# An adaLN block on one core: the scale columns loaded ahead of the shift columns, the first key projection in token halves, eight single PSUM banks, and a new written-out order

## The chip, the core and the metric

The kernel runs on one core of a Trainium2 chip. The metric is the time of one execution on the device in microseconds; the number given for a kernel is the median of several runs. A profile is one execution taken by the hardware profiler; its span runs from the first to the last instruction of the program. TensorE is called PE below, VectorE DVE, ScalarE ACT, GpSimd POOL, and SyncE, which issues most of the DMAs here, SP.

## What is computed

```python
def reference(A_x, A_wqkv, A_wo, B_x, B_w1, B_b1, B_w2, B_b2, c, w_mod):
    def _A_ref(x, wqkv, wo):          # H = 32 heads of 16, W = 8 keys, dilation 2
        q, k, v = split(x @ wqkv)
        idx = pos[:, None] - off[None, :]            # off = 0, 2, .., 14
        logits = einsum('bhsd,bhswd->bhsw', q, k[idx]) * scale   # idx < 0 masked
        o = einsum('bhsw,bhswd->bhsd', softmax(logits), v[idx])
        return o.reshape(B, S, D) @ wo
    def _B_ref(x, w1, b1, w2, b2):    # mixes tokens: S = 2048, F = 1792
        u = gelu(einsum('bsd,sf->bdf', layernorm(x), w1) + b1)
        return transpose(einsum('bdf,fs->bds', u, w2) + b2)
    mod = silu(c) @ w_mod             # six rows of 512: sa, ca, ga, sb, cb, gb
    h = layernorm(x) * (1 + ca) + sa
    x = x + ga * _A_ref(h, A_wqkv, A_wo)
    h = layernorm(x) * (1 + cb) + sb
    return x + gb * _B_ref(h, B_w1, B_b1, B_w2, B_b2)
```

x is 2048 x 512 in bfloat16, wqkv 512 x 1536, wo 512 x 512, w1 2048 x 1792, w2 1792 x 2048, w_mod 512 x 3072.

## The kernel before

The 2048 tokens are worked in four chunks of 512 (`build_chunk`, L562), each of four tiles of 128 tokens. Nothing is scheduled while the kernel runs: the function records some 670 operations in a graph (`_Graph`, L98), and the string `ORDER` (L27) names them one by one. An engine gets its operations in the order in which their names stand there, and works them off strictly in that order; a suffix chooses the engine where an operation has alternatives (`:v` DVE, `:a` ACT, `:g` POOL), and a digit the PSUM buffer where it takes one. So where an operation waits, all later ones of that engine wait behind it. The order of names of different engines against each other means nothing on the chip. A `dur` beside an operation, such as 0.95 for `gmul` on POOL (L548), is the author's number and isn't used when the program runs.

The operations of chunk n, by the names that the text uses:

- `ln1s`, `rstd1_n`, `nb1_n`, `ln1n`: statistics of the first layernorm by tile of 128 tokens (`ln1s0` to `ln1s15`), the reciprocal deviation, minus mean times it, and the normalized tile. `nb1_n` and `ln1n` may run on POOL. An `ln1n` on ACT or POOL needs `nb1_n`.
- `tr`, `hT`: PE transposes the normalized tiles into PSUM; the eviction multiplies by 1 + ca and adds sa (`a1col`, `sacol`).
- `qkvk`, `qkvq`, `qkvv` and `evk`, `evq`, `evv`: projections, and their evictions to SBUF.
- `vd`: 16 SP DMAs copy the values into the shifted layout.
- `qk` (four per chunk): DVE multiplies queries and eight shifted keys, 4096 elements per partition, both inputs from SBUF. `red` sums over the head's elements on PE with column tiles, `max` (DVE, from PSUM), `sub` (PE), `exp` (ACT), `sum` (PE), `rb` (ACT), `smul` (DVE) finish the softmax.
- `a2`, `a2ev`, `pv` (four, like `qk`, DVE, both inputs from SBUF), `pvacc` (PE, column tiles), `oev`: the weighted values.
- `wo`, `x1ev`, `x1sq`: output projection per tile, with the residual. It needs `woq` multiplied by the row ga: `bc0` (SP) spreads the row over the partitions into `ga_bc`, and `gmul0` to `gmul3` multiply the four 512-wide parts of `woq` (L545 to L551), each on DVE or on POOL.
- `t`, `aff`, `ln3s`, `h3`: second layernorm, its scale and shift, and the third layernorm. `t` and `h3` may run on POOL.

Then `mlp1` multiplies by w1 in two halves of tokens (the first half is parked in SBUF, `park`, and is ready after two chunks, so its matmuls fill PE's time during chunks 2 and 3), `gadd`, `gelu` and `gbm` follow, and `mlp2`, `xb`, `fin` and `st_out` finish.

At the start, two DMAs, `ld_wmodA` and `ld_wmodB`, bring the columns of both sa and ca of w_mod by halves of rows (L413, L414). `modcols0` and `modcols1` multiply them with silu(c), and `modcols_cp` writes `sacol` and `a1col` (L482 to L503). `warm0` to `warm4` are 21 matmuls whose results nobody reads. PSUM is four tiles of two banks each (L273); an operation that fills one bank still holds both. Eight semaphores are shared by all DMAs of SP and ACT, so the issue of a DMA waits for the landing of the eighth one before it.

Of the kernel before, what the change touches and what calls it, by code (L numbers as in the profile page):

```python
# [27 lines left out]
consts ld_x00 consts2 ld_c warm0:0 ld_x02 ld_wmodA act_table ld_wmodB ld_w1a ld_x1a cps:1 warm1:2 ld_w1b silu_exp  # L28
ln1s0:v ld_x1b ln1s1:a ld_x2 ld_w0 silu_dve halo0 warm2:3 ln1s2:v rstd1_0_0 ln1s3:v modcols0:0 nb1_0_0:v ln1n0:v
warm3:1 rstd1_0_2 ln1n1:v nb1_0_2:v ln1n2:v modcols1 ln1n3:v tr0_00:2 tr0_10:3 modcols_cp:a tr0_02 tr0_12 hT0_0:a  # L30
warm4:1 hT0_1:v hT0_3:v qkvk0_0:0 hT0_2:v sc_rep ln1s7:v ln1s4:v ln1s9:v ln1s8:v ln1s11:v ln1s10:v qkvk0_1:1 qkvk0_2:3
qkvk0_0b qkvk0_1b ln1s5:a ln1s6:a rstd1_1_0 evk0_1:a nb1_1_0:g qkvq0_1:2 qkvq0_0:1 evk0_2:a evk0_0:a evq0_1:a ln1n7:a
evq0_0:a ln1n6:g ln1n4:g ln1n5:v qk0_1 qk0_0 qkvq0_2:3 ld_wo3 ld_wmod2 ld_w2 ld_wo1 ld_wmod3 ld_x3 ld_wmod4 ld_wmod5
ld_wo2 khalo1 ld_wo0 evq0_2:a tr1_10:0 tr1_00:2 qkvv0_0:1 qkvv0_2:3 hT1_0:a hT1_1:a hT1_3:a hT1_2:a evv0_0:a evv0_2:a
rstd1_2_0 vd0_010 vd0_030 vd0_020 vd0_120 vd0_000 vd0_021 vd0_001 vd0_031 vd0_100 vd0_101 vd0_131 vd0_011 vhalo1
vd0_130 ld_b2 vd0_111 vd0_121 vd0_110 qkvk1_0:0 qkvq1_0:2 red0_0:1 qk0_2 qk0_3 nb1_2_0:v red0_1 red0_2 red0_3 ln1s13:v
ln1s12:v max0 qkvq1_2:3 sub0 ln1n10:g ln1n11:g ln1n8:g evk1_0:a ln1s15:a ln1n9:a evq1_0:a ln1s14:a rstd1_3_0 evq1_2:a
exp0 qkvk1_2:0 modrows:2 tr2_10:3 sum0 evk1_2:a mrow_ev rb0 qk1_1 qk1_0 qk1_3 smul0 nb1_3_0:v qk1_2 tr2_00:0 qkvv1_0:2
a2_0:1 hT2_0:a hT2_1:a hT2_2:a ln1n12:a a2ev0:a evv1_0:a hT2_3:a ln1n15:a ln1n13:a ln1n14:a pv0_0 pv0_1 qkvv1_2:0
red1_0:1 red1_1 red1_2 red1_3 qkvq2_0:2 tr3_00:3 evv1_2:a evq2_0:a hT3_0:a bc0 khalo2 vd1_030 vd1_120 vd1_020 vd1_021  # L40
vd1_010 vd1_000 vd1_001 vd1_100 vd1_031 vd1_110 vd1_011 vd1_131 vd1_130 vd1_111 vd1_121 vd1_101 pvacc0_0:0 pvacc0_1
qkvk2_0:2 max1 pv0_3 pv0_2 oev0_1:a hT3_2:a sub1 tr3_10:0 qkvv2_0:3 evk2_0:a exp1 sum1 pvacc0_2:2 hT3_1:a rb1 hT3_3:a
gmul3:g gmul0:v gmul2:v gmul1:v qk2_1 smul1 qk2_0 pvacc0_3 qkvv2_2:1 oev0_3:a evv2_0:a evv2_2:a wo1:0 a2_1:2 x1ev1:a
a2ev1:a pv1_0 pv1_1 wo3:3 wo0:1 wo2:0 x1ev3:a x1sq1 x1sq3 x1ev0:a x1ev2:a qkvk2_2:2 pvacc1_0:3 qkvq2_2:1 pvacc1_1
x1sq2 evk2_2:a x1sq0 rstd2_0_0 evq2_2:a pv1_2 nb2_0_0:v pv1_3 t0:v qk2_3 qk2_2 qkvq3_0:0 pvacc1_2:2 pvacc1_3 qkvk3_0:1
t2:a t3:a oev1_1:a evq3_0:a oev1_3:a t1:a wo6:3 wo7:0 wo5:2 evk3_0:a x1ev6:a vhalo2 ld_b1 bc2 ld_w1_0_1 khalo3 bc1
vd2_101 ld_w1_0_2 vd2_000 ld_w1_0_0 vd2_131 vd2_121 vd2_010 vd2_001 vd2_030 vd2_031 ld_w1_0_3 vd2_020 red2_0:1 red2_1
wo4:3 x1sq6 x1ev7:a x1ev5:a x1sq7 x1sq5 x1ev4:a x1sq4 rstd2_1_0 red2_2 red2_3 aff0_0 qk3_1 ln3s0_1:v nb2_1_0:v
ln3s0_3:a max2 ln3s0_0:v ln3s0_2:v qkvv3_2:0 qkvk3_2:2 sub2 t4:a t7:g t6:g t5:g evv3_2:a exp2 rstd3_0_0 evk3_2:a
aff1_0 nb3_0_0:v qkvv3_0:3 biascols:0 sum2 qkvq3_2:2 rb2 h3_3:a evv3_0:a evq3_2:a ln3s1_2:a ln3s1_3:a h3_1:g h3_0:g  # L50
ln3s1_0:v biascols_cp ln3s1_1:v h3_2:v qk3_0 smul2 qk3_2 rstd3_1_0 mlp1_0_30_0:1 mlp1_0_31_0 mlp1_0_10_0:0 mlp1_0_11_0
a2_2:3 red3_0:2 red3_1 a2ev2:a nb3_1_0:v qk3_3 h3_6:a h3_4:a h3_5:a h3_7:v red3_2 mlp1_0_00_0:3 mlp1_0_01_0 red3_3
# [24 lines left out]
st_out14_0 st_out15_384
# [20 lines left out]
class _Graph:  # L98
# [11 lines left out]
    def slot(self, pool):  # L110
        return _Slot(pool)
# [36 lines left out]
    def schedule(self):  # L148
# [3 lines left out]
        for tok in ORDER.split():  # L152
            name, _, how = tok.partition(":")
            o = by[name]
            if how and how[0].isalpha():
                o.eng, o.dur, o.fn = next(a for a in o.alts if a[0] == ENGINES[how[0]])
                how = how[1:]
            assert done.issuperset(o.deps), name
            for s_ in o.use:
                if s_.first == o.idx:  # L160
                    s_.i = int(how)
                    assert busy[s_.pool][s_.i] is None, name
                    busy[s_.pool][s_.i] = s_
# [68 lines left out]
def kernel(  # L232
# [14 lines left out]
    WARM=(4, 4, 4, 5, 4),  # L247
# [63 lines left out]
    sacol = T([P, KT], F32, "sacol")  # L311
# [669 lines left out]
```

## Time and profile before

| | |
|---|---|
| median of 3 runs | 198.21 us (198.18 to 198.45) |
| the profiled execution, span | 197.0 us |
| what lies around the span in the median | 1.2 us |
| DVE, ACT, POOL busy over the span | 153.5, 123.4, 18.0 us |
| first matmul, end of the last one | 1.4 us, 194.1 us |
| granted TensorE clock, mean | 0.998 |

How to read it: a row of a timeline gives the start, the duration of the whole group, engine, line, operation, tiles written and read, shapes, and the number of instructions; the bracket is the idle time of the engine before it and what ended it. All operations pass through one helper, so that nearly every row has its line, L184, and is told apart by its tiles: `ps<-hTb,w_q` is a query projection, `prod<-q_sb,k_c`, `gT<-q_sb,k_c` and `h<-q_sb,k_c` are `qk`, `pvb<-a2sb,vD` is `pv`, `ee<-ps` is `exp`, `ps<-ee,ident` is `sum`, `ee<-ee,rb` is `smul`, `woq<-woq,ga_bc` is `gmul`, `n_sb<-xx,...` is `ln1n`, `junk<-xx` with `junk<-xx,mv` is `ln1s` on ACT, and `h<-h,...` is `h3`. Matmuls are pipelined, so a PE row overlaps the next one; the distance of starts is what counts.

### The profile page before, as it was taken

What the parts mean: (1) busy time and instruction counts of PE and PEld (TensorE: products, weight loads), DVE (VectorE), ACT (ScalarE), POOL (GpSimd) and SP (SyncE); (2) the same over time, 40 slices, a digit from 0 to 9 for tenths busy, and PEclk for the clock granted to TensorE, in tenths of its full rate; (3) what the DMA queues carried; (4) which work ended last, traced back from release to release, by engine and by line L of the source; (5) the groups of instructions that cost most, each with busy time, mean ns of one, the idle gap of its engine ahead of it and who ended that gap; (6) DMA issues with size and microseconds to landing.
All of it is one profiled execution on the core that took longest, in us unless ns stands there. A gap on an engine that the chain in (4) does not pass through costs nothing.

```text
span 197.0 us, 3408 instructions
## 1 busy us (share of the span) xinstructions
PE 190.1 (97%) x1289; PEld 88.2 (45%) x1289; DVE 153.5 (78%) x198; ACT 123.4 (63%) x242; POOL 18.0 (9%) x46
## 2 busy tenths in 40 slices
PE   7889999999999999999999999999999999999994
PEld 2546545445443435433434444444444444444452
DVE  1699989999999999999999999928776127261463
ACT  5498999999999999993769999917541000000000
POOL 7003040090000004300000011000000000000000
PEclk9999999999999999999999999999999999999999
DMA  6999978507994994693999999990000871720112
GB/s 182 369 312 318 302 195 177 120 14 180 171 196 99 270 201 84 187 289 106 174 206 290 234 295 292 292 273 4 0 0 0 229 200 68 199 81 26 57 53 80
DMA packets 45348, 33.59 MB, mean 171 GB/s; under 512 B 5396, under 2 KB 42772, under 8 KB 45332
## 3 DMA queue, kind: packets, MB, share of 16 engines
q1 hardware_dynamic: 44908, 32.82, 67.2%
q10 hardware_dynamic: 424, 0.56, 1.0%
q8 instruction: 10, 0.16, 0.4%
q14 instruction: 6, 0.05, 0.1%
HBM read 22.03 MB, written 2.10 MB: 122 GB/s over the span
## 4 chain that ended last, share of the span: by engine, by line
PE 64%; DVE 12%; DMA 11%; ACT 5%; SPq 3%; issue 2%; ACTq 0%; DVEq 0%
PE ps L184 64%; DMA vD<-v_c 5%; DMA w_q<-in_A_wqkv_dram 4%; SPq L184 3%; DVE pvb L184 3%; DVE prod L184 3%; DMA vD<-in_w_mod_dram 3%; DVE st L184 2%; ACT n_sb L184 1%; DVE h L184 1%; ACT hTb L184 1%; DVE gT L184 1%; ACT v_c L184 1%; DVE ee L184 1%; DVE nm L184 1%
## 5 line engine op out<-in xcount | busy, mean ns | idle before, releaser
L184 DVE TENSOR_TENSOR pvb<-a2sb,vD 128x4096 bf16<-128x4096 bf16 x16 | 36.0, 2284 | 0.2 <-issue 0.2
L184 PE MATMUL ps<-h,wst 128*128 128x512 bf16 x128 | 29.5, 379 | 0.0
L184 DVE TENSOR_TENSOR prod<-q_sb,k_c 128x4096 bf16<-128x4096 bf16 x9 | 20.4, 2285 | 0.1
L184 PEld LDWEIGHTS <-wst 128*128 128x128 bf16 x128 | 12.1, 98 | 16.0 <-issue 1.7
L184 PE MATMUL ps<-gT,vD 128*128 128x512 bf16 x84 | 19.1, 379 | 0.0
L184 PE MATMUL ps<-hTb,w_q 128*128 128x512 bf16 x64 | 15.1, 381 | 1.0 <-DMA w_q<-in_A_wqkv_dram 0.7
L184 DVE TENSOR_TENSOR q_sb<-ps,q_sb 128x512 bf16<-128x512 f32 x8 | 5.4, 687 | 13.6 <-PE ps L184 13.6
L184 PE MATMUL ps<-woq,o_sb 128*128 128x512 bf16 x64 | 15.8, 379 | 0.0
L184 PEld LDWEIGHTS <-w_q 128*128 128x128 bf16 x96 | 9.9, 109 | 12.6 <-issue 2.5
L184 PE MATMUL ps<-hTb,w_v 128*128 128x512 bf16 x64 | 15.0, 380 | 0.0
L184 PE MATMUL ps<-hTb,w_k 128*128 128x512 bf16 x64 | 15.0, 380 | 0.0
L184 DVE TENSOR_TENSOR k_c<-ps,k_c 128x512 bf16<-128x512 f32 (+2 forms) x9 | 5.6, 629 | 11.7 <-PE ps L184 11.7
L184 PEld LDWEIGHTS <-o_sb 128*128 128x128 bf16 x106 | 9.7, 98 | 10.5 <-issue 0.4
L184 PEld LDWEIGHTS <-vD 128*128 128x128 bf16 x116 | 9.2, 97 | 11.4 <-DMA vD<-in_w_mod_dram 1.5
L184 PE MATMUL ps<-gT,pvb 128*128 128x512 bf16 x56 | 12.9, 379 | 0.0
L184 PEld LDWEIGHTS <-w_k 128*128 128x128 bf16 x80 | 8.7, 111 | 8.9 <-issue 0.8
L184 PE MATMUL ps<-gT,prod 128*128 128x512 bf16 x56 | 12.2, 379 | 0.0
L184 PEld LDWEIGHTS <-w_v 128*128 128x128 bf16 x80 | 8.3, 111 | 8.2 <-issue 1.3
L184 ACT ACTIVATE junk<-xx,su 128x512 bf16<-128x512 bf16 x16 | 11.5, 720 | 0.5 <-DVE xx L184 0.2
L184 DVE BATCH_NORM_STATS2 st<-xx 128x6 f32<-128x512 bf16 x11 | 7.4, 671 | 4.7 <-DMA xx<-in_A_x_dram 4.7
L184 ACT ACTIVATE hTb<-ps,sacol,a1col 128x512 bf16<-128x512 bf16 x13 | 9.6, 782 | 0.5 <-PE ps L184 0.5
L184 DVE TENSOR_TENSOR gT<-q_sb,k_c 128x4096 bf16<-128x4096 bf16 x4 | 9.1, 2284 | 0.0
(113 smaller groups left out, 315.1 us busy)
## 6 DMA issues: line engine op xcount, KB each, us to landing
vD<-v_c SPq DMA_DIRECT2D x64, 131.5 KB, 4.6
wst<-in_B_w_dram SPq DMA_DIRECT2D x8, 512.0 KB, 6.1
vD<-in_B_w_dram SPq DMA_DIRECT2D x3, 896.0 KB, 7.3
wst<-in_w_mod_dram SPq DMA_DIRECT2D x4, 512.0 KB, 9.3
prod<-in_B_w_dram SPq DMA_DIRECT2D x2, 896.0 KB, 11.0
pvb<-in_B_w_dram SPq DMA_DIRECT2D x2, 896.0 KB, 8.1
xx<-in_A_x_dram SPq DMA_DIRECT2D x4, 256.0 KB, 4.7
xx<-in_A_x_dram SPq DMA_DIRECT2D x2, 512.0 KB, 7.7
```

Of the source, the lines that this page charges most:

```text
L184: r = fn(*a, **k)
```

## The change

- The columns of ca are loaded by themselves, in two halves right behind x (`ld_ca0`, `ld_ca1`), then the key weights (`ld_wk0`, `ld_wk2`), and then the columns of sa in one piece (`ld_sa`). `colsa` and `a1_cp` give `a1col`, `colss` and `sa_cp` give `sacol`.
- For chunk 0 the eviction of the transposes only multiplies by `a1col` (`hk`, by halves of 256 tokens). The keys are projected from that, with the contraction outermost: for each half and each quarter of the contraction four matmuls of 256 columns go to four banks (`qkvk0_kt_half`). The shift's share of the keys is 16 matmuls of one column (`kbias`), and is added as a bias when the keys are evicted (`evk0_0` to `evk0_3`). For queries and values `hadd` adds `sacol` to the multiplied tile.
- PSUM is one tile of eight banks; an operation takes one, two or (the keys of chunk 0) four separate banks.
- The 21 matmuls of `warm` become 16.
- `ORDER` is new from end to end, and so are the choices of engine. POOL gets 36 operations beside the constants instead of 14 (`halo0` left out): ten `ln1n` instead of five, four `gmul` instead of one, nine `t` instead of three, seven `h3` instead of three, six `nb` instead of two. ACT gets ten `ln1s` instead of five.

What four engines get around the softmax of chunk 0 and of chunk 1, each row one engine's own order:

```
before ACT:  ... evk1_2 mrow_ev rb0 hT2_0 hT2_1 hT2_2 ln1n12 a2ev0 evv1_0 hT2_3 ln1n15 ln1n13 ln1n14 evv1_2 evq2_0 hT3_0 oev0_1 hT3_2 evk2_0 exp1 ...
after  ACT:  ... mrow_ev evk1_2 exp0 hT2_1 hT2_3 rb0 hT2_0 hT2_2 a2ev0 evv1_0 evv1_2 rstd1_3_0 evq2_0 evk2_0 ln1n12 oev0_1 exp1 evv2_2 ln1n15 rb1 ...
before DVE:  ... max0 qk1_1 qk1_0 qk1_3 smul0 nb1_3_0 qk1_2 pv0_0 pv0_1 max1 pv0_3 pv0_2 gmul0 gmul2 gmul1 qk2_1 smul1 ...
after  DVE:  ... qk1_0 max0 qk1_1 qk1_3 smul0 qk1_2 pv0_0 pv0_1 max1 pv0_2 pv0_3 qk2_1 smul1 qk2_0 pv1_0 ...
before POOL: ... ln1n10 ln1n11 ln1n8 gmul3 t7 t6 t5 ...
after  POOL: ... nb1_2_0 ln1n8 ln1n9 ln1n11 ln1n10 gmul1 gmul2 gmul3 nb1_3_0 ln1n13 gmul0 ln1n14 t0 t1 t2 t3 nb2_1_0 ...
after  PE:   ... sum0 tr2_00 qkvv1_2 a2_0 qkvq2_0 qkvk2_0 red1_0 .. red1_3 pvacc0_0 pvacc0_1 qkvv2_2 sub1 qkvv2_0 sum1 qkvq2_2 ...
```

The code, cut to its core:

```diff
-    WARM=(4, 4, 4, 5, 4),
+    WARM=(4, 4, 2, 3, 3),
...
-    NPS = 4
-    ps = [psp.tile([P, 2, 512], F32, name=f"ps{i}") for i in range(NPS)]
+    NPS = 8
+    ps = psp.tile([P, NPS, 512], F32, name="ps")
...
     def bank(s_, h):
-        return ps[s_.i][:, h, :]
+        return ps[:, s_.i + h, :]
...
-    dma(wmodA[:, 0:2, :], wmod_view[:, 0:2, 0:2 * D], 2 * D * P * 2 * 2, [], vdk[0][4:], "ld_wmodA", "act")
-    dma(wmodA[:, 2:4, :], wmod_view[:, 2:4, 0:2 * D], 2 * D * P * 2 * 2, [], vdk[0][:4], "ld_wmodB")
+    for kh in range(2):
+        dma(wmodc[1][:, 2 * kh:2 * kh + 2, :], wmod_view[:, 2 * kh:2 * kh + 2, D:2 * D], D * P * 2 * 2, [],
+            vdk[0][2 * kh:2 * kh + 2], f"ld_ca{kh}", "act" if kh == 0 else "sp")
...
+    for a in (0, 2):
+        load_w(1, a, a + 2, f"ld_wk{a}")
+    dma(wmodc[0], wmod_view[:, :, 0:D], KT * D * P * 2, [], vdk[0][4:], "ld_sa")
+    load_w(0, 0, 4, "ld_wq")
+    load_w(2, 0, 4, "ld_wv")
...
+    def f_kb():
+        for j in range(4):
+            for kt in range(KT):
+                nc.tensor.matmul(bank(sl_kb, 0)[:, j:j + 1], lhsT=_ap(w_p[1][:, kt, j:j + 1], [[4, P]]),
+                                 rhs=sabf[:, kt:kt + 1], start=(kt == 0), stop=(kt == KT - 1), skip_group_check=True)
...
+            for (g0, g1) in parts:
+                for kt in range(KT):
+                    def f(kt=kt, g0=g0, g1=g1):
+                        for j in range(4):
+                            nc.tensor.matmul(bank(sk[j], 0)[:, g0 * P:g1 * P], lhsT=_ap(w_p[1][:, kt, j:j + 1], [[4, P]]),
+                                             rhs=hraw[:, kt, g0 * P:g1 * P], start=(kt == 0), stop=(kt == KT - 1))
...
+                G.add_any([("act", _act(C), lambda j=j, dst=dst: nc.scalar.activation(
+                                dst, bank(sk[j], 0), ACT.Identity, bias=kbcol[:, j:j + 1])),
```

More of the change, by code (lines that the diff above doesn't have):

```diff
@@ L38 @@
[L38 to L52, printed above, removed]
@@ L598, in build_chunk @@
                     writes=[(stp[kp], g0)], name=f"tr{ch}_{kp}{g0}", lat=0.15, use=[stp[kp]])
[L599 to L609 removed]
+        hraw = gT[:, 2:6, :]
@@ L624, in build_chunk @@
         for (t, j0, j1) in plan:
[L625 removed]
             n = j1 - j0
[L628 to L638 removed]
+            sq = G.slot("ps", n)
```

289 lines of the change are left out of this document (175 added, 114 removed).

## The prediction, made before the changed kernel ran

> **What bounds the kernel now.** First the busy sums by engine, then stretches of 10 us, then the start of PE's timeline beside the chain of waits.
>
> ```profile
> PE 190.1 (97%) x1289; PEld 88.2 (45%) x1289; DVE 153.5 (78%) x198; ACT 123.4 (63%) x242; POOL 18.0 (9%) x46
> ```
> ```profile
> 30.00:40.00 10.00, 9.61 (x122) 5.13 (x124) 10.00 (x7) 9.80 (x18) 1.03 (x1) 1.00 0.62 134
> 40.00:50.00 10.00, 9.91 (x99) 5.23 (x88) 10.00 (x9) 9.53 (x15) 4.23 (x1) 1.00 0.47 109
> ```
>
> The columns of the stretches are length, PE, its weight loads, DVE, ACT and POOL in us, then clock, DMA share, GB/s. PE is the bound, but from 30 to 50 us DVE has no idle time and ACT little: here three engines set the pace together, and what delays one delays PE soon. POOL alone is free, and the change gives it 36 operations for 14.
>
> ```profile
> 8.23 0.54 PE L184 MATMUL ps<-sc,vD 128*128 128x1 bf16 x16
> 8.64 1.05 PE L184 MATMUL ps<-ident,n_sb 128*128 128x128 bf16 x16
> ...
> 10.40 3.61 PE L184 MATMUL ps<-hTb,w_k 128*128 128x512 bf16 x16
> 14.70 3.65 PE L184 MATMUL ps<-hTb,w_q 128*128 128x512 bf16 x16 [0.69 <-DMA w_q<-in_A_wqkv_dram]
> ```
> ```profile
> 1.38 5.32 DMA vD<-in_w_mod_dram
> ...
> 6.71 7.94 DMA w_q<-in_A_wqkv_dram
> ```
>
> The second fence is the chain: the first w_mod load holds the semaphore that w_q's issue waits for, and the queries start when w_q lands. So the start is bound by loads; from 14.70 PE hardly pauses.
>
> **The start.** Ahead of w_q the queue carried x0 (0.5 MB), both w_mod halves (1.0), w_k (0.5), x1 (0.5) and x2 (0.5). The new order puts x2 behind w_q: 0.5 MB less, and the bandwidth there prices it.
>
> ```profile
> 5.00:10.00 5.00, 4.31 (x61) 2.69 (x60) 3.17 (x9) 2.30 (x10) 0.00 (x0) 1.00 1.06 368
> 10.00:15.00 5.00, 4.31 (x21) 2.07 (x20) 4.86 (x13) 4.87 (x15) 0.53 (x3) 1.00 1.11 310
> ```
>
> 0.52 MB at 310 to 368 GB/s is 1.4 to 1.7 us, so w_q lands near 13.1. But PE must get there.
> ```profile
> 3.45 0.69 DVE L184 BATCH_NORM_STATS2 st<-xx 128x6 f32<-128x512 bf16 x1 [3.45 <-DMA xx<-in_A_x_dram]
> ```
> ```profile
> 3.44 0.17 ACT L184 ACTIVATE ecol<-ps 128x4 f32<-128x4 f32 x1 [0.33 <-PE ps L184]
> 3.65 0.44 ACT L184 ACTIVATE ecol<-ecol 128x4 f32<-128x4 f32 x2
> ```
>
> x is there at 3.45 as before. ACT's silu, 0.65 in all, now stands behind a statistics pair (1.5, below) and a reciprocal (0.7 estimated, being three small operations like silu's): it ends at 6.3. DVE finishes the first two tiles, then silu's product, by 6.8; `colsa` runs to 7.2, a statistics pair on DVE (0.9) stands ahead of `a1_cp`, the first `hk` ends near 8.1, and the keys start at 8.2 (10.40 before). The second tile pair is normalized only by 9.4, because its ACT statistics stand behind silu and end at 7.9, with a reciprocal and three DVE operations to follow. With the transposes waiting for that, `colss` (0.4), `kbias` (16 one-column matmuls, like the rows of 16 in 0.41 from 8.23 to 8.64) and 32 half-length matmuls (3.5), the keys end at 13.6. Queries start at 13.6: **-1.1 us**, with bounds -1.7 (PE ready when w_q lands) and 0 (`sa`, which stands ahead of the last part of the first key half in PE's order, lands late). The five dropped warm matmuls lie in waiting time: 0.
>
> **ACT ahead of the first softmax.** ACT's own order decides when `exp0` runs.
>
> ```profile
> L184 ACT ACTIVATE hTb<-ps,sacol,a1col 128x512 bf16<-128x512 bf16 x13 | 9.6, 782 | 0.5 <-PE ps L184 0.5
> ```
> ```profile
> 10.24 0.62 ACT L184 ACTIVATE junk<-xx 128x512 bf16<-128x512 bf16 x1
> ...
> 11.83 0.63 ACT L184 ACTIVATE junk<-xx 128x512 bf16<-128x512 bf16 x1
> ...
> 31.49 1.01 ACT L184 ACTIVATE ee<-ps 128x1024 bf16<-128x1024 f32 x1
> 32.40 1.02 ACT L184 ACTIVATE k_c<-ps 128x1024 bf16<-128x1024 f32 x1
> ```
>
> A statistics pair takes 1.5 (10.24 to 11.83), an eviction of 1024 takes 0.9 (31.49 to 32.40), an `hT` 0.7 (9.6 for 13), and I give an `ln1n`, of the same width, the same. Between the landing of x1 and `exp0` ACT gets four more pairs (+6.1), two `ln1n` and three `hT` fewer (-3.5), three evictions of chunk 0's keys and queries fewer or smaller (-1.4), one reciprocal less (-0.5), and `mrow_ev` and `evk1_2`, which stood behind (+1.5): +2.2, and it starts this stretch 0.6 later. `exp0` then ends at 32.5 + 2.8 = 35.3. PE reaches `sum0` (33.41 before) with `qkvv1_0` (1.7) put ahead of it at 33.4 + 1.7 - 1.1 = 34.0. **+1.3 us**, bounds 0 and 2.5. The start's gain is mostly gone here.
>
> **`gmul` and `nb1_3` on POOL.** This step makes the forecast.
>
> ```profile
> 25.90 2.27 POOL L184 TENSOR_SCALAR n_sb<-xx,rs,nb 128x512 bf16<-128x512 bf16 x3 [9.48 <-DVE nb L184]
> 38.97 5.25 POOL L184 TENSOR_TENSOR woq<-woq,ga_bc 128x512 bf16<-128x512 bf16 x1 [10.80 <-DMA ga_bc<-mrow]
> ```
> ```profile
> 36.52 2.28 DVE L184 TENSOR_TENSOR gT<-q_sb,k_c 128x4096 bf16<-128x4096 bf16 x1
> 38.72 4.49 DVE L184 TENSOR_TENSOR pvb<-a2sb,vD 128x4096 bf16<-128x4096 bf16 x2
> 43.13 1.22 DVE L184 TENSOR_REDUCE nm<-ps 128x128 bf16<-128x1024 f32 x1
> ```
>
> The one `gmul` on POOL took 5.25 us, while an operation of the same width with one tensor input takes 0.77 (25.90, three in 2.27). It became ready 0.25 us after DVE had begun two `pv`, and ended 1.0 us after the second of them (44.22 against 43.21), when DVE had gone over to a reduction from PSUM. I read it as 4.2 us of waiting and 1.0 of work: POOL doesn't get at SBUF while DVE runs one operation with two SBUF inputs behind the other, not even at the seam at 40.9. The other reading, 5.25 us of plain work, makes the following worse.
>
> The Trainium skill's page "SBUF — State Buffer", section "Who interferes with whom", states that a DVE instruction with two SBUF inputs and a GpSimd instruction that reads SBUF exclude each other for the whole instruction, and that the one that starts first blocks the other. The trace agrees in this one place, with 5.25 us.
>
> Before, nobody waited for that row. Now POOL's order is `gmul1 gmul2 gmul3 nb1_3_0 ln1n13 gmul0 ln1n14`, and ACT's `ln1n12` needs `nb1_3_0`; behind `ln1n12` on ACT stand `oev0_1` and `exp1`, for `exp1` waits `sum1` on PE, and for `rb1` behind it `smul1` on DVE.
>
> ```profile
> 36.04 0.62 SPq L184 DMA_DIRECT2D ga_bc<-mrow  x1
> ```
>
> When: `mrow_ev` ends at 33.4 (35.3 less `exp0` and `evk1_2`), and from issue to use ga_bc took 2.9 (36.04 to 38.97): ready at 36.4, a little issue time included. DVE ends `qk1_3` at 36.5 and waits for `rb0` to 37.3, so `gmul1` gets in and ends at 37.55. Then DVE runs `smul0`, `qk1_2`, `pv0_0`, `pv0_1` in a row to 44.8 (0.6 and 3 x 2.2, as from 36.52 to 38.72). `gmul2` runs beside `max1` (1.1), `gmul3` perhaps at its end, then come `pv0_2`, `pv0_3`, `qk2_1`, which wait for nothing: to 52.5, or 53.5 where `gmul3` went first. DVE now stops at `smul1`, and only here `nb1_3_0` gets in; done at 53.7. ACT has from 35.3: four `hT` 2.8, `rb0` 0.6, `a2ev0`, two `evv1`, `evq2_0`, `evk2_0` 4.6, a reciprocal 0.5. It stands at `ln1n12` from 43.8, ten us. Then `ln1n12`, `oev0_1`, `exp1` take 2.6: 56.3.
>
> ```profile
> 33.41 0.61 PE L184 MATMUL ps<-ee,ident 128*128 128x128 bf16 x8
> ...
> 46.69 1.89 PE L184 MATMUL ps<-hTb,w_v 128*128 128x512 bf16 x8
> 48.41 0.61 PE L184 MATMUL ps<-ee,ident 128*128 128x128 bf16 x8
> 48.95 1.05 PE L184 MATMUL ps<-pvb,stack 128*32 128x512 bf16 x16
> 49.93 1.92 PE L184 MATMUL ps<-hTb,w_v 128*128 128x512 bf16 x8
> ```
>
> PE, from `sum0` at 35.4, has five projections of 1.73 (46.69 to 48.41), `red1` and two `pvacc` (six column-tiled groups, 48.95 to 49.93 being two: 2.9), `sum0`, `tr2_00`, `a2_0` and `sub1` (0.3 to 0.5 each: 1.6), and 0.5 of small waits: it stands at `sum1` from 49.0 to 56.3. **+7.3 us.** Bounds: 0.6 where `nb1_3_0` is done by 47, beside `max1`, since `exp1` then ends at 49.6; +9.3 where `gmul1` misses its gap and two more `gmul` have to run at the end. I take 7.3, because every operation of DVE in that row has its inputs.
>
> **Second layernorm on POOL.** `t0` to `t3` and `h3_0` to `h3_3` become 0.77 each, in series on one engine.
>
> ```profile
> 117.95 0.77 POOL L184 TENSOR_SCALAR h<-h,rs,nb 128x512 bf16<-128x512 bf16 x1
> ```
> ```profile
> 7.28 1.43 DVE L184 TENSOR_SCALAR n_sb<-xx,mv,rs 128x512 bf16<-128x512 bf16 x4
> ...
> 118.19 0.99 DVE L184 TENSOR_SCALAR h<-h,mv,rs 128x512 bf16<-128x512 bf16 x2
> ```
>
> At 0.77 as here and at 25.90, four cost 3.1 us in series. The second row's kind takes DVE 0.36 each; the pair at 118.19, begun beside POOL's row of 117.95, took 0.99, so 0.27 went to waiting: these operations exclude DVE's too, if briefly. Beside `qk` or `pv` none ran. `aff0_0` and the first `mlp1` follow; lower bound 0 (both hidden by ACT's queue), upper +4.3 (ready behind a `qk`, 2.2 each for `ln1n6` and for `t0`). I take **+1.0**.
>
> **The rest.** PE changes between full and column-tiled matmuls cost 0.09 to 0.12: `sum1` is eight starts of 0.056 and ends at 48.86, `pvacc` begins at 48.95. The old order has 40 such changes, the new one 28: 12 x 0.095 is **-1.1**. One PSUM tile for eight banks gives no new wait by the order of instructions (every wait on it is for the last reader of the same bank): 0; cover gone, it would be an eviction of 0.9 each time. The tail is again a 128-column matmul, one `fin` and a store: 0, within 0.2.
>
> Sum on the profiled span: 197.0 - 1.1 + 1.3 + 7.3 + 1.0 - 1.1 = 204.4; with the 1.2 around it **205.6 us**. Its own range, from the bounds, which don't all fall to one side: 202.5 to 209.
>
> **The rivals.** (a) *POOL gets in.* A late `a2ev0` or `red1` leaves DVE idle for two us before `max1`, and `nb1_3_0` is done by 47: 198.2 - 1.1 + 1.3 - 1.1 = 197.3, and 196.0 to 196.5 where ACT keeps up too. For it: `a2ev0` comes only about half a us before DVE wants it. Against it: two us of idleness are needed in an engine that had none from 30 to 50. Faster. (b) *Everything on POOL waits behind DVE's two-input operations*, `ln1n6` and the `t` and `h3` included: 205.6 + 3.3 = 208.9. For it: the rows at 118.19. Against it: no single-input row ran beside a `qk` or `pv`. The page named above says that it holds for any GpSimd read, so it would give this time. (c) *Half a stall*: `nb1_3_0` gets in after `pv0_2` or `pv0_3`, 2.2 to 4.4 us earlier: 201 to 203.5. (d) *The load order does nothing*, because the queries still wait for w_q at 14.7 (it is again among the last loads), and POOL is harmless: 198.2 within 0.3.
>
> **How the numbers follow.** Forecast 0.47, (a) 0.22, (b) 0.14, (c) 0.13, (d) 0.04. Under 0.2% counts as no change, about what a measurement of this kernel can tell. Faster 0.22, same 0.04, slower 0.74. The range reaches into (a) and (b): 196.2 to 209.2.
>
> **What would show it.** First query matmul at 13.6 (start). A gap of one to two us at `sum0`, ended by ACT's `exp0`. POOL rows of `gmul` of several us each between 36 and 55, ending where DVE idles or reduces. ACT idle for about ten us before `n_sb`, released by POOL's `nb`; PE idle for about seven before the second `sum`. If POOL's `gmul` rows take about 1 us beside `qk` and `pv`, or `ln1n12` waits for less than two us, the forecast is wrong and (a) is right. If PE's second `sum` starts by 50 and the time is still long, the loss lies in the second layernorm.

## The result and the profile after

The changed kernel takes 213.74 us (median of four runs, 211.87 to 215.03); the kernel before, run beside it, 198.33. The ratio is 1.0745 with an interval of 1.0663 to 1.0826: slower by about 15 us, where 205.6 was forecast and the range ended at 209.2. The profiled execution is the shortest of the four: a span of 210.2 us against 197.0. The profiled executions of x5 and x6 began with a late first load of w_mod (PE waited 2.0 and 3.2 us for it, 0.7 before), so they are read for their rows and not for their spans.

First the busy sums and one of the stretches, with the columns as before (length, PE, its weight loads, DVE, ACT, POOL, clock, DMA share, GB/s).

```profile
PE 193.7 (92%) x1318; PEld 91.6 (44%) x1318; DVE 159.8 (76%) x190; ACT 121.7 (58%) x254; POOL 59.2 (28%) x72
```
```profile
40.00:50.00 10.00, 7.28 (x67) 3.01 (x65) 10.00 (x5) 6.14 (x9) 9.67 (x6) 0.96 0.65 164
```

POOL is busy for 59.2 us instead of 18.0, and DVE, which gave work away, for 159.8 instead of 153.5, in fewer instructions (190 for 198). From 40 to 50 us PE and ACT have the idle time now, and DVE still has none. So something lengthens DVE's own operations. POOL's and DVE's timelines of that stretch show what.

```profile
38.54 7.47 POOL L187 TENSOR_TENSOR woq<-woq,ga_bc 128x512 bf16<-128x512 bf16 x3 [5.36 <-DMA ga_bc<-mrow]
45.98 2.24 POOL L187 TENSOR_TENSOR nb<-mv,rs 128x4 f32<-128x4 f32 x1
...
49.52 3.18 POOL L187 TENSOR_TENSOR woq<-woq,ga_bc 128x512 bf16<-128x512 bf16 x1
52.69 5.44 POOL L187 TENSOR_SCALAR n_sb<-xx,rs,nb 128x512 bf16<-128x512 bf16 x1
```
```profile
38.60 3.24 DVE L187 TENSOR_TENSOR gT<-q_sb,k_c 128x4096 bf16<-128x4096 bf16 x1
41.77 6.39 DVE L187 TENSOR_TENSOR pvb<-a2sb,vD 128x4096 bf16<-128x4096 bf16 x2
48.09 1.21 DVE L187 TENSOR_REDUCE nm<-ps 128x128 bf16<-128x1024 f32 x1
49.22 5.63 DVE L187 TENSOR_TENSOR pvb<-a2sb,vD 128x4096 bf16<-128x4096 bf16 x2
```

The `qk` at 38.60 takes 3.24 us and the two `pv` behind it 6.39; before, the same rows had 2.28 and 4.49. The three `gmul` end at 46.01, and each of the three DVE operations is 0.95 to 0.97 us too long, the time that one `gmul` works. So the two engines take turns: a POOL operation waits until the running DVE operation ends, and then the next DVE operation waits until POOL has worked. The maximum at 48.09, which reads PSUM, is not lengthened (1.21, before 1.22). The Trainium skill's page "SBUF — State Buffer", section "Who interferes with whom", makes the shared port pair an exclusive lock for which a DVE instruction with two SBUF inputs and a GpSimd instruction that reads SBUF contend, and says that issue order decides who blocks and that a reduction never contends. The trace agrees, with 0.96 us for a `gmul` and, for the 512-wide operations with one tensor input, 0.19 to 0.50.

PE's timeline shows what the lengthened DVE rows do to it.

```profile
13.60 1.89 PE L187 MATMUL ps<-hTb,w_q 128*128 128x512 bf16 x8
...
20.91 0.96 PE L187 MATMUL ps<-ident,n_sb 128*128 128x128 bf16 x14 [1.47 <-POOL n_sb L187]
...
48.22 0.61 PE L187 MATMUL ps<-pvb,stack 128*32 128x512 bf16 x8 [2.54 <-DVE pvb L187]
48.76 3.28 PE L187 MATMUL ps<-hTb,w_v 128*128 128x512 bf16 x8
...
54.36 0.61 PE L187 MATMUL ps<-ee,ident 128*128 128x128 bf16 x8
...
90.00 5.30 PE L187 MATMUL ps<-h,wst 128*128 128x512 bf16 x16 [3.00 <-POOL h L187]
```
```profile
48.70:52.70 4.00, 4.00 (x15) 1.53 (x12) 4.00 (x3) 1.59 (x2) 3.92 (x3) 0.57 1.13 162
90.00:94.00 4.00, 4.00 (x11) 1.51 (x11) 4.00 (x7) 3.33 (x9) 0.00 (x0) 0.57 1.18 298
```

The queries start at 13.60, but PE stands three times for something that DVE or POOL delivers late: `ln1n6` at 20.91, the second `pv` at 48.22, `h3` at 90.00. (A fourth pause, 1.50 us at 141.25, is left for further down.) After the two longer pauses the granted clock is 0.57 in the mean of four us: eight matmuls of a projection take 3.28 us there instead of 1.89.

ACT's timeline has the wait that the forecast named:

```profile
48.57 0.81 ACT L187 ACTIVATE n_sb<-xx,nb,rs 128x512 bf16<-128x512 bf16 x1 [3.76 <-POOL nb L187]
```

ACT stands 3.76 us at `ln1n12` for `nb1_3_0`; a dozen us before it had ended `exp0` at 35.93.

A sum over DVE's row, from the start of the first `qk` to the end of the last `pv`, sorts the loss. The two ends come from these rows; "blocked" is what the operations of the row take beyond the median of their own form in the profiles of before and of x4 (a form that neither has counts as it is), "idle" the time between operations, "work" the rest. The last column is the end of the last matmul less the end of the last `pv`.

```profile
17.67 2.54 DVE L187 TENSOR_TENSOR prod<-q_sb,k_c 128x4096 bf16<-128x4096 bf16 x1
...
120.77 2.28 DVE L187 TENSOR_TENSOR pvb<-a2sb,vD 128x4096 bf16<-128x4096 bf16 x1
```

| us | first qk | work | blocked | idle | last pv ends | to the last matmul's end |
|---|---|---|---|---|---|---|
| before | 16.67 | 92.6 | 0.5 | 1.7 | 111.52 | 82.57 |
| changed | 17.67 | 90.9 | 7.7 | 6.8 | 123.05 | 84.01 |

The last matmul ends 13.0 us later. 11.5 of it is DVE's row: 1.0 a later start, 7.2 blocked by POOL (3.8 of it by the four `gmul`), 5.1 more idle time, less 1.7 us of work that POOL really took over. The new idle time stands at three places of DVE's row. Two of them are these:

```profile
21.97 1.00 DVE L187 TENSOR_SCALAR hTb<-ps,a1col,sacol 128x512 bf16<-128x512 bf16 x2 [1.60 <-PE ps L187]
...
76.59 1.23 DVE L187 TENSOR_TENSOR h<-h,ab_bc 128x2048 bf16<-128x2048 bf16 x1 [1.80 <-POOL h L187]
```

The first waits for the transposes behind `ln1n6`, the second is `aff0_0`, which waits for the `t` of chunk 0 on POOL. The third, 1.85 us ahead of the `pv` at 97.79, is for ACT's `a2ev2`, which comes behind PE's pause for `h3`. So each leads back to POOL. The other 1.4 us lie behind the last `pv`. There PE waits 1.50 us at 141.25 for DVE's last `h3`, which had waited 1.06 us for ACT's reciprocal deviation; the kernel before has no pause of PE's of 0.9 us or more there.

### The profile page after: what moved, and what is told of

Read it like the earlier page. It is cut to its first block, busy times and chain, and to the rows that moved or that the text cites. A ratio compares the mean times of both kernels' runs of the same rounds, so it can differ in the third digit from the quotient of the medians.

```text
span 210.2 us, 3500 instructions
## 1 busy us (share of the span) xinstructions
PE 193.7 (92%) x1318; PEld 91.6 (44%) x1318; DVE 159.8 (76%) x190; ACT 121.7 (58%) x254; POOL 59.2 (28%) x72
## 4 chain that ended last, share of the span: by engine, by line
PE 45%; DMA 14%; POOL 12%; ACT 11%; SPq 8%; DVE 5%; issue 2%; POOLq 0%; ACTq 0%; DVEq 0%
PE ps L187 45%; SPq L187 8%; ACT junk L187 6%; POOL woq L187 5%; DMA woq<-in_A_wo_dram 5%; DMA vD<-in_B_w_dram 5%; DVE h L187 4%; DMA vD<-in_w_mod_dram 3%; POOL n_sb L187 3%; POOL h L187 2%; POOL nb L187 2%; DMA ga_bc<-mrow 2%; ACT xx L187 1%; ACT lv L187 1%; ACT o_sb L187 1%
## 5 line engine op out<-in xcount | busy, mean ns | idle before, releaser
L187 DVE TENSOR_TENSOR pvb<-a2sb,vD 128x4096 bf16<-128x4096 bf16 x16 | 39.1, 2477 | 1.9 <-ACT a2sb L187 1.9
L187 PE MATMUL ps<-h,wst 128*128 128x512 bf16 x128 | 31.6, 395 | 4.5 <-POOL h L187 3.0
L187 POOL TENSOR_SCALAR n_sb<-xx,rs,nb 128x512 bf16<-128x512 bf16 x10 | 22.6, 2272 | 0.5 <-POOL nb L187 0.2
L187 DVE TENSOR_TENSOR prod<-q_sb,k_c 128x4096 bf16<-128x4096 bf16 x9 | 21.9, 2434 | 0.1
L187 POOL TENSOR_SCALAR h<-h,rs,nb 128x512 bf16<-128x512 bf16 x7 | 7.3, 1054 | 40.7 <-DVE nb L187 40.6
L187 PE MATMUL ps<-hTb,w_v 128*128 128x512 bf16 x64 | 16.5, 405 | 0.0
L187 PEld LDWEIGHTS <-w_k 128*128 128x128 bf16 x112 | 10.6, 112 | 8.0 <-issue 1.7
L187 POOL TENSOR_SCALAR h<-xx,rs,nb 128x512 bf16<-128x512 bf16 x9 | 9.2, 1036 | 13.6 <-DVE nb L187 13.4
L187 POOL TENSOR_TENSOR woq<-woq,ga_bc 128x512 bf16<-128x512 bf16 x4 | 10.7, 2684 | 5.4 <-DMA ga_bc<-mrow 5.4
L187 PE MATMUL ps<-pvb,stack 128*32 128x512 bf16 x128 | 9.1, 382 | 3.0 <-DVE pvb L187 3.0
```

The costliest lines, as they stand in the source:

```text
L187: r = fn(*a, **k)
```

## The experiments

**x1: the four `gmul` back on DVE.**

```diff
- ... smul0 gmul1:g ... gmul2:g gmul3:g ... nb1_3_0:g ln1n13:g gmul0:g qk1_2 ... pv0_2 pvacc0_2:2 pv0_3 qk2_1
+ ... smul0 ... nb1_3_0:g ln1n13:g qk1_2 ... pv0_2 pvacc0_2:2 pv0_3 gmul1:v gmul2:v gmul3:v gmul0:v qk2_1
```


> The changed kernel with its four gmul on DVE, behind pv0_3, instead of on POOL; all else as changed. Theory A (POOL and DVE take turns at SBUF: each gmul on POOL holds up the DVE operation behind it by about 1 us, and PE waits for DVE): qk1_2, pv0_0 and pv0_1 go back from 3.2 to 2.3 us each, PE's stall of 2.5 us at the second pvacc and the slow clock after it go, DVE pays 1.3 us later: 209.3 to 210.8. Rival B (POOL alone waits, what hurts is that ACT stands for nb1_3_0): nb1_3_0 still waits for DVE to leave its row, ACT still stands over 3 us, 212 to 214. Rival C (the new order of PE or ACT's longer list is what costs): 213.5.

Measured 208.11 us, ratio 1.0454 (1.0396 to 1.0512): 5.6 us less than the changed kernel, where theory A asked for 2.9 to 4.4. DVE's and PE's timelines of x1:

```profile
40.23 4.48 DVE L187 TENSOR_TENSOR pvb<-a2sb,vD 128x4096 bf16<-128x4096 bf16 x2
...
50.59 1.42 DVE L187 TENSOR_TENSOR woq<-woq,ga_bc 128x512 bf16<-128x512 bf16 x4
```
```profile
54.86 0.42 PE L187 MATMUL ps<-ee,selB 64*32 64x128 bf16 x32 [1.77 <-DVE ee L187]
```

The first two `pv` are back at 4.48 us, and PE's wait between the two `pvacc` is gone. Four `gmul` cost DVE 1.42 us here; on POOL they had cost it 3.8. The price is paid a little later: `smul1`, which now stands behind them, lets PE wait for 1.77 us. ACT waits 0.79 us for `nb1_3_0` and PE for nothing behind it: rival B had it wait for over 3 us still, and falls as it was put. But DVE's hold and ACT's wait went together here, so x1 doesn't say how much of the 5.6 us belongs to each.

**x2: part of the third layernorm off POOL.**

```diff
- nb3_0_0:g ... h3_2:g h3_3:g h3_1:g h3_0:g
+ nb3_0_0:v ... h3_2:a h3_3:a h3_1:v h3_0:v
```


> The changed kernel with nb3_0_0, h3_0 and h3_1 on DVE and h3_2 and h3_3 on ACT instead of on POOL; the rest as changed. Theory A: PE's stall of 3.0 us ahead of the first mlp1 falls under 1 us and the slow clock of 3.9 us at 0.56 after it goes, which is worth 1.7 us more: 209.5 to 211. Rival (the first mlp1 would wait for aff0_0 or aff1_0 on DVE and the third statistics anyway): above 212.5.

Measured 215.34 us, ratio 1.081 (1.0757 to 1.0862): no gain; theory A was wrong. The rival's number holds, though not its reason. PE's timeline of x2:

```profile
92.38 2.75 PE L187 MATMUL ps<-h,wst 128*128 128x512 bf16 x12 [0.99 <-ACT k_c L187]
97.31 1.05 PE L187 MATMUL ps<-prod,group 128*32 128x512 bf16 x16 [2.18 <-DVE prod L187]
```

The wait for POOL's `h` at the first `mlp1` is gone, and in its place PE waits for ACT's `evk3_2` (0.99) and for DVE's `qk3_0` (2.18), which the four operations had pushed back. Work taken off POOL lands on engines that have no room at that place.

**x3: PE's pauses filled.**

```diff
-    WARM=(4, 4, 2, 3, 3),
+    WARM=(4, 4, 2, 3, 3, 10, 12),
- pvacc0_1 ... mlp1_0_00_0:6
+ warm5:3 pvacc0_1 ... warm6:6 mlp1_0_00_0:6
```


> The changed kernel with 10 matmuls that nobody reads ahead of the second pvacc and 12 ahead of the first mlp1, where PE stands still; nothing else is changed, and the stalls themselves stay. If the low granted clock after the two stalls (0.56 and 0.57 over 3.9 us) comes from the pause and PE's pace sets the end: the clock stays 1.00 there and the time falls by 1.7 to 3.4 us, 210.3 to 212. If other engines set the pace behind the stalls: 213 to 214, with the clock at 1.00. If the low clock has nothing to do with the pause: clock still 0.56, 213.7.

Measured 213.74 us, ratio 1.0742 (1.0698 to 1.0786): the time of the changed kernel. The stretches of x3 behind the two filled pauses, and the one after a pause of 3.13 us at 57 that was not filled:

```profile
48.80:53.70 4.90, 3.69 (x18) 1.77 (x16) 4.90 (x3) 2.68 (x4) 4.76 (x2) 1.00 1.08 170
60.40:64.40 4.00, 4.00 (x53) 1.98 (x54) 2.02 (x1) 2.97 (x6) 0.00 (x0) 0.68 0.01 4
93.80:98.00 4.20, 4.13 (x28) 1.80 (x31) 4.20 (x7) 3.40 (x9) 0.02 (x1) 1.00 1.19 293
```

The clock is 1.00 behind the filled pauses and low behind the open one, so the low clock does come from the pause; and keeping it up leaves the time where it was. In the first of these stretches PE is again idle for 1.2 us of 4.9, and PE's timeline of x3 says why:

```profile
53.71 0.61 PE L187 MATMUL ps<-ee,ident 128*128 128x128 bf16 x8 [1.21 <-ACT ee L187]
...
60.37 0.51 PE L187 MATMUL ps<-ident,n_sb 128*128 128x128 bf16 x6 [3.13 <-POOL n_sb L187]
```

It now waits at `sum1` for `exp1`, which stands behind `ln1n12` and `nb1_3_0`, and then for POOL's `ln1n14`. The second outcome of the expectation holds: behind the stalls other engines set the pace.

**x4 and x8: the new start with the old order behind it.** x4 takes the changed kernel's names up to the eviction of chunk 0's keys and then those of before, each PSUM tile of two banks as a pair of single ones. x8 differs from it in this (behind it, banks 2 and 6 trade places):

```diff
- evk0_3:v evk0_0:v ln1s9:v ln1s8:v ln1s11:v ln1s10:v rstd1_1_0 evk0_2:a evk0_1:a ... qkvq0_1:6 ... qkvq0_2:2
+ ln1s9:v ln1s8:v ln1s11:v ln1s10:v rstd1_1_0 evk0_1:a qkvq0_1:1 ... evk0_0:a ... evk0_2:a evk0_3:a ... qkvq0_2:6
```


> The changed kernel's code and its order up to the eviction of chunk 0's keys (loads, key halves, bias, eight single banks), and from there the order and the choices of engine of before. If the start's 1.1 us are real and the rest of the change only loses: 197.0 to 197.4. If the four more statistics pairs on ACT in the start push the first softmax back: 198 to 199. If the eight single banks or the new start cost by themselves: above 199.

> As x4_start_only, with two of the four evictions of chunk 0's keys moved from DVE to ACT, the last query projection of chunk 0 in a bank that the keys don't hold, and the statistics of chunk 2 on DVE right behind the shift. If DVE's row sets the pace: its first qk moves from 18.7 to about 17.0 us and the time falls by as much, 198.1 to 198.9. If PE sets the pace: 199.5 to 200.2 unless the stall ahead of the transposes goes too. If ACT, with 1.2 us more to do, is late for the transposes: over 199.5 with the first qk at 17.

Measured 200.14 us for x4, ratio 1.0065 (1.004 to 1.0091), and 199.50 for x8, 1.0051 (1.0025 to 1.0077). Both are slower than before, by less than 1%. PE's and DVE's timelines of x4, then DVE's of x8:

```profile
13.26 1.89 PE L186 MATMUL ps<-hTb,w_q 128*128 128x512 bf16 x8
```
```profile
18.70 2.28 DVE L186 TENSOR_TENSOR prod<-q_sb,k_c 128x4096 bf16<-128x4096 bf16 x1
```
```profile
17.64 2.29 DVE L186 TENSOR_TENSOR prod<-q_sb,k_c 128x4096 bf16<-128x4096 bf16 x1
```

In x4 PE starts the queries 1.4 us earlier than before, and DVE the first `qk` 2.0 us later: the four `hadd` and two evictions of keys stand in DVE's order ahead of it, and the statistics follow them. x8, with less on DVE, begins it 1.1 us earlier than x4 and has its last `pv` 0.5 us earlier in its profile. The ratios differ by 0.3 us only, inside their intervals, where 1.7 was expected of a start at 17.0: 199.50 stands at the edge of the outcome in which PE sets the pace. So the time doesn't follow the first `qk` us for us. The distance from the last `pv` to the last matmul is 82.57 and 82.56 us, that of before, so eight single banks, used in pairs, cost nothing there.

**x5 and x6: POOL loaded in the kernel before.** x5 adds eight operations that nobody waits for; x6 moves three `gmul` over.

```diff
+                if st == 8:
+                    for k in range(8):
+                        add("pool", 0.78, lambda: nc.gpsimd.tensor_scalar(
+                            scr[:], xx[:, 8, :], rs[0][0][:, 0:1], nb[0][0][:, 0:1], op0=ALU.mult, op1=ALU.add),
+                            reads=[("xx", 8), rk, nk], writes=["scr"], name=f"scr{k}")
```
```diff
- gmul3:g gmul0:v gmul2:v gmul1:v qk2_1
+ gmul3:g gmul0:g gmul2:g gmul1:g qk2_1
```


> The kernel before, with eight more operations on POOL behind ln1n8, at 28.2 us: each normalizes the same tile of 128x512 into a scratch tile that nobody reads; no instruction of another engine waits for them. Theory A (turns at SBUF, and DVE's row from the first qk to the last pv sets the pace): those that meet a qk or pv hold DVE for 0.3 to 0.45 us each and wait some 2 us themselves, gmul behind them holds it for 0.96: DVE blocked by 2 to 4 us, the last pv and the end later by as much, 200.3 to 202.3. Rival B (only POOL waits, as the prediction had it): DVE not blocked, 198.2 to 198.8. Rival C (DVE blocked, but PE sets the pace): 198.5 to 199.3.

> The kernel before with all four gmul on POOL instead of one; DVE loses three operations of 0.34 us. Theory A: the three hold DVE for 0.96 us each, unless one falls beside a maximum: DVE's last pv is 0.9 to 1.9 us later, 199.4 to 200.4. Rival B (only POOL waits): DVE saves 1.0 us, 197.4 to 198.5.

x5 measured 203.57 us, ratio 1.0235 (1.0191 to 1.0278), x6 a ratio of 1.0102 (1.006 to 1.0145), 2.0 us more than before. POOL's and PE's timelines of x5, then POOL's and DVE's of x6:

```profile
30.58 28.59 POOL L183 TENSOR_SCALAR scr<-xx,rs,nb 128x512 bf16<-128x512 bf16 x8
59.14 1.15 POOL L183 TENSOR_TENSOR woq<-woq,ga_bc 128x512 bf16<-128x512 bf16 x1
```
```profile
60.33 0.58 PE L183 MATMUL ps<-woq,o_sb 128*128 128x512 bf16 x1 [4.97 <-POOL woq L183]
```
```profile
44.09 11.43 POOL L183 TENSOR_TENSOR woq<-woq,ga_bc 128x512 bf16<-128x512 bf16 x4 [11.25 <-DMA ga_bc<-mrow]
```
```profile
48.12 6.39 DVE L183 TENSOR_TENSOR pvb<-a2sb,vD 128x4096 bf16<-128x4096 bf16 x2
54.43 3.24 DVE L183 TENSOR_TENSOR prod<-q_sb,k_c 128x4096 bf16<-128x4096 bf16 x1
```

Eight operations of 0.77 us work, 6.2 in all, took POOL 28.6 us beside DVE's row, and held it by 0.2 to 0.4 us at six places. They cost more than expected; in the profile `gmul` queued behind them and the output projection waited 4.97 us for it. That execution took 209.28 and the other three 202.72 to 203.82, so not each of them need have this wait in full. In x6 three operations of DVE are 0.95 to 0.96 us longer: for each `gmul` that DVE no longer does in 0.36 us (1.42 for four in x1) it now waits 0.96. Rival B falls here too, without anything of the change's order or start.

**x7: the new order with the old engines.** Behind the start each operation stands on the engine that it had before. It keeps its new place, except that the four `gmul` stand behind `pv0_3`, and `nb1_3_0`, `ln1n13` and `ln1n14` behind `pv0_0`.

```diff
- ln1n7:g ln1n9:g ln1n13:g t1:g t2:g t3:g h3_3:g ... t0:g nb1_3_0:g gmul0:g ... ln1s12:a ln1s13:a
+ ln1n7:a ln1n9:a ln1n13:a t1:a t2:a t3:a h3_3:a ... t0:v nb1_3_0:v gmul0:v ... ln1s12:v ln1s13:v
...
```


> The changed kernel with its start and its order of names, but behind the start every operation on the engine that it had before (gmul behind pv0_3 on DVE, nb1_3_0 behind pv0_0). It tells the order alone from the choice of engine. Theory A: DVE blocked under 1 us instead of 7.7 over its row; the row's work is that of before and some idle time stays: 200 to 204. If the new order of PE costs most of it by itself: 206 or more.

Measured 223.11 us, ratio 1.1238 (1.1194 to 1.1283). DVE is blocked for 1.4 us only over its row, and idle for 15.5; behind the last `pv` 88.0 us stand instead of 82.6. The waits of PE and of DVE in x7:

```profile
PE ps L187 <- DVE prod L187: 4.2, 1, 4.2
```
```profile
DVE nb L187 <- ACT rs L187: 12.0, 7, 5.2
```

The columns are total, times and longest. DVE stands for ACT's reciprocal deviations, and PE for a `qk` of DVE's that comes late by them: I read from this that the new order counts on ACT not having these operations. The number is that of the second outcome (206 or more), but the waits shown lead to ACT, not to PE's order by itself. The run does not tell the order from the choice of engine; it says that they hold only together.

**x9: POOL only writes.**

```diff
-                nc.gpsimd.tensor_tensor(nb_t, mean_t, rs_t, op=ALU.mult)
-                nc.gpsimd.tensor_scalar(nb_t, nb_t, k, None, op0=ALU.mult)
+                nc.gpsimd.memset(nb_t, 0.0)
...
-                ("pool", 0.78, lambda: nc.gpsimd.tensor_scalar(dst, src, rs_ap, nb_ap, op0=ALU.mult, op1=ALU.add))]
+                ("pool", 0.78, lambda: nc.gpsimd.memset(dst, 0.5))]
...
-                       ("pool", 0.95, lambda q_=q_: nc.gpsimd.tensor_tensor(woq[:, q_, :], woq[:, q_, :], ga_bc[:],
-                                                                            op=ALU.mult))],
+                       ("pool", 0.95, lambda q_=q_: nc.gpsimd.memset(woq[:, q_, :], 0.5))],
```


> The changed kernel with the same order and the same operations on POOL, but each of POOL's 36 (minus means, normalizations, gmul) only fills its output tile with a constant: it reads nothing from SBUF and waits for no input, so the output isn't the reference's. What stays is the new start, the new order and the longer lists of ACT and DVE. If all of the loss comes from POOL reading SBUF beside DVE: DVE blocked under 0.5 us, the last pv near 112, 197 to 199. If about half of it does, and the rest is the start and the order: DVE blocked under 0.5 us, 200 to 205. If writing alone holds DVE too: blocked by several us, above 207.

Measured 201.64 us, ratio 1.0156 (1.0114 to 1.0198). Groups of x9 (busy us and mean ns of one; then idle time and releasers):

```profile
L187 DVE TENSOR_TENSOR pvb<-a2sb,vD 128x4096 bf16<-128x4096 bf16 x16 | 36.0, 2285 | 0.0
...
L187 POOL MEMSET n_sb<- 128x512 bf16 x10 | 4.9, 525 | 20.3 <-PE ps L187 17.9 <-DVE st L187 2.4
```
```profile
L187 DVE TENSOR_TENSOR pvb<-a2sb,vD 128x4096 bf16<-128x4096 bf16 x16 | 39.1, 2477 | 1.9 <-ACT a2sb L187 1.9
```

The second fence is the same group of the changed kernel: 2477 ns for a `pv`, and 2285 when POOL only writes. Writing takes 0.525 us and blocks nothing: DVE's row is blocked for 1.1 us in all, no operation of it by more than 0.21. (The Trainium skill's page "SBUF — State Buffer", section "Who interferes with whom", says that a DVE instruction with two SBUF inputs contends with a GpSimd instruction that reads SBUF, not with one that only writes it; the trace agrees.) DVE's row begins at 17.91, 1.2 us later than before, the last `pv` ends at 113.7, and 83.1 us stand behind it; PE's pause ahead of its last `mlp1` half, 1.29 us here, stays, so that one is not POOL's. So some 12 of the 15 us hang on POOL's reading beside DVE and on what waits for POOL, and 3.3 us remain with the start, the longer ACT list and the order. x9 takes away the hold on DVE and the waits for POOL at once and doesn't part the 12. Even with a POOL that costs DVE next to nothing the changed kernel is not faster than before.

**x10: the changed kernel again.**

> The changed kernel once more, for a second profile: its runs lie up to 3 us apart, the first profile was of the fastest of them. If chance at the seams between DVE's operations decides when a waiting POOL operation gets in: DVE blocked by 6 to 9 us again, but other POOL operations wait longest, and a PE stall of 3 us for n_sb near 60 us may stand where the first profile has 0.5. 211.5 to 215.

Measured 214.01 us, ratio 1.0784 (1.0741 to 1.0828). PE's timeline in this profile, whose execution took 215.1:

```profile
53.25 0.61 PE L187 MATMUL ps<-ee,ident 128*128 128x128 bf16 x8 [1.46 <-ACT ee L187]
...
59.91 0.82 PE L187 MATMUL ps<-ident,n_sb 128*128 128x128 bf16 x6 [3.13 <-POOL n_sb L187]
```

Here the last `gmul` and `ln1n14` got in later, PE waits 3.13 us for that tile, and 1.46 us for `exp1`. DVE's row is blocked for 6.4 us and idle for 11.4. The two profiles, of executions of 211.87 and 215.1 us, part where `ga_bc` lands: in the first `gmul1` is ready at 38.54 and meets the seam between `smul0` and `qk1_2`; here it is ready at 39.05, when `qk1_2` has begun at 38.51, and all that stands behind it on POOL comes later. Whether a waiting operation then gets in at the next seam stays open: in the first profile a `gmul` got in at each seam, a normalization at 23.37 waited for the running `qk`, let two more pass and ended 7.0 us later, and the one `gmul` of before let one `pv` pass.

**x11 and x12: more work on PE alone, on DVE alone.** In the kernel before, ten matmuls that nobody reads (`warm5`, ahead of `qkvv2_2`), and six normalizations into a scratch tile on DVE (ahead of `qk2_1`).

```diff
- pvacc0_3 qkvv2_2:1
+ pvacc0_3 warm5:1 qkvv2_2:1
```
```diff
- gmul3:g gmul0:v gmul2:v gmul1:v qk2_1
+ gmul3:g gmul0:v gmul2:v gmul1:v scr0 scr1 scr2 scr3 scr4 scr5 qk2_1
```


> The kernel before, with ten more matmuls of 512 columns that nobody reads, 2.13 us of PE's time, ahead of qkvv2_2 at 49.9 us, where PE doesn't wait. If DVE's row sets the pace and PE has time to spare: 198.2 to 199.2. If PE, which has few pauses, sets it together with DVE: 2.1 us more, 200.2 to 200.8.

> The kernel before, with six more normalizations of a 128x512 tile into a scratch tile on DVE ahead of qk2_1 at 49.7 us, 0.32 to 0.34 us each, 2.0 us in all. If DVE's row sets the pace: the last pv and the end 1.9 to 2.1 us later, 200.1 to 200.7. If PE sets it: 198.2 to 199.2.

x11 measured 201.19 us, ratio 1.0102 (1.0062 to 1.0142), 2.0 us more; x12 201.28, ratio 1.0129 (1.0076 to 1.0182), 2.6 us more. DVE's timeline of x11, then PE's of x12:

```profile
57.79 6.70 DVE L183 TENSOR_TENSOR pvb<-a2sb,vD 128x4096 bf16<-128x4096 bf16 x3 [1.98 <-ACT a2sb L183]
```
```profile
54.29 0.42 PE L183 MATMUL ps<-ee,selB 64*32 64x128 bf16 x32 [2.25 <-DVE ee L183]
```

Each delay shows up on the other engine within ten us: 2.13 us of matmuls become 1.98 us of idle DVE at `pv1_0`, two us on DVE become 2.25 us of idle PE behind `smul1`. Neither has time to spare, so a loss on DVE's row is a loss at the end, and from the last `pv` to the last matmul all kernels with the old order have 82.6 us, also these two. A version faster than the kernel before was not found; x8 comes nearest.

## Why the prediction came out as it did

The direction was right, and so was the place: the row of DVE around `gmul` and `nb1_3`, and POOL's part in the second layernorm. That the direction came out is in part luck, for the wait that was to give +7.3 hardly shows, and another cost stands at the same place.

The 8 us that were missed lie in two parts. What depends on POOL was forecast at +8.3 (7.3 and 1.0), and x9 prices it at some 12. The other three terms, -1.1, +1.3 and -1.1, came to -0.9, and x9, where POOL hardly holds DVE, still measured +3.3. In the first part the step that failed is that POOL alone waits: its hold on DVE was put at nothing, and DVE's row was blocked for 7.2 us. In the second it is above all the start, forecast at -1.1 and measured at 1.3 to 1.6 in x4, with the sign wrong.

*`gmul` and `nb1_3` on POOL, +7.3.* The step let DVE run "`smul0`, `qk1_2`, `pv0_0`, `pv0_1` in a row to 44.8" and made POOL alone wait. The row ended at 48.09, because each `gmul` got in at a seam and held DVE for 0.96 us (x6 shows the same; in x1, without them, the hold is gone). The one `gmul` of before could not show that: it happened to work beside a maximum. But the row at 118.19, with 0.27 us of waiting on DVE, was in hand, and was called brief and left out of the sum; the Trainium skill's sentence that either blocks the other was quoted, and priced on one side only, in rival (b) as well, whose 208.9 was therefore too low. `ga_bc` also came 2.1 us later than the 36.4 worked out, and the gap in DVE ahead of `smul0` in which `gmul1` was to run wasn't there; it got in all the same. Since POOL did get in, `nb1_3_0` was done at 48.5 and not at 53.7, beside `max1` as in rival (a) but 1.5 us later than its 47; ACT stood for 3.8 us, not ten, and PE reached `sum1` at 54.36, not 56.3. The chain that the forecast named, `nb1_3_0` to `exp1` to `sum1`, is there in x10 and x3 with 1.2 to 1.5 us. In the first profile PE's stall for `pv`, 2.54 us, and the slow matmuls behind it cover it. As a price for four `gmul` on POOL the 7.3 was not too low, for x1 gives 5.6; the rest of the 12 belongs to the other operations of POOL (6.5 us from x1 to x9, of which 1.4 is the work of the `gmul` that x1 has on DVE). Of their single-input kind the forecast priced only those of the second layernorm.

*The start, -1.1.* Queries at 13.6 were forecast and came at 13.60. But the gain was booked as PE's, and PE's queries alone say little: DVE begins the first `qk` at 17.67 instead of 16.67, and x4 shows a loss of about 1.3 to 1.6 us from the new start under the old order. The step counted no DVE work for `hadd` and the evictions of keys. By their first `qk` x4 is 2.0 us later than before and x8 1.0, by their ratios they cost 1.3 and 1.0: the late `qk` goes with the loss, but is not shown to be all of it. The bounds of -1.7 and 0 left the true sign out.

*ACT ahead of the first softmax, +1.3.* `exp0` was to end at 35.3 and ended at 35.93. No gap stood at `sum0`, though: PE came there no sooner, having lost 1.47 us for `ln1n6` at 20.91, again POOL beside a `qk`, which the forecast had only in rival (b) and in an upper bound.

*Second layernorm, +1.0.* Mis-sized: PE's wait ahead of the first `mlp1` was 3.00 us, and DVE stood 1.80 us for `t`. x2 shows that this is not POOL's alone to give back.

*The rest.* The slow clock after pauses was not foreseen; x3 shows that it did not add to the time here. The tail was put at 0; behind the last `pv` the changed order takes 84.0 us instead of 82.6, with PE's pause of 1.50 us in it, and with free POOL (x9) 83.1. The 1.1 us for fewer changes between full and column tiles was not tried by itself. One PSUM tile was put at 0, and x4 and x8 show no cost of it with banks in pairs; the new order's own use of single banks was not tried by itself.

As a whole, the forecast summed stalls of PE. That is sound only with the delays of the engine beside it in the sum: DVE's row had as little slack as PE (x11, x12), and 7.2 us of blocking went into it.

## What to carry to other kernels

Moving an operation to an idle engine is not free if the two engines take turns at SBUF: price it on both sides, its wait on the new engine and the hold that it puts on the old one. Here a `gmul` cost DVE 0.36 us when DVE did it, and 0.96 when POOL did. An idle engine can still take work that falls beside PSUM reads or that only writes; and before booking an earlier start on one engine, look at the first operation of every other engine that has no slack.

## What the runs showed of the hardware

POOL operations that wait for SBUF don't get in at every seam between two DVE operations: a `gmul` waited for one `qk` or `pv` (changed) or for two `pv` (before), a normalization for one `qk` (at 18.05) or for three (at 23.37). The runs of the changed kernel differ by 3 us; how much of that this makes isn't shown, for the runs of before spread too, by 2.5 us beside x1 to x4 (198.16 to 200.65).

The granted clock fell to 0.50 for 3.4 us behind PE's pauses of 2.54 and 3.00 us (from 49.16 and from 90.12 on, which makes the means of 0.57 over four us), behind one of 3.13 in x10, and in x2 behind one of 2.18 that had another of 0.99 ahead of it; behind one of 2.73 us in x1 it stayed at 1.00. The stretch of x1 behind it:

```profile
86.30:90.30 4.00, 3.99 (x25) 1.69 (x27) 4.00 (x7) 3.36 (x9) 0.00 (x0) 1.00 1.15 277
```

The Trainium skill's page "TensorE: Matmul & The Clock Gate", Part 1, gives half rate after an idle window of some 3.4 us that runs freely; by these rows a pause of 2.5 us can be enough, and a somewhat longer one need not be.
